# First head group of an attention and FFN kernel: keys and queries in two loads each, scores and exponentials by pairs of heads

## The chip, the cores and the metric

The kernel runs on one core of a Trainium2 chip. The metric is the device time of one execution in microseconds (us). Three executions of the kernel before took 380.77, 381.61 and 380.28; the median is 380.77.

The engines of the core go by these names in the profile: PE is TensorE (matmuls; PEld are its weight loads), DVE is VectorE, ACT is ScalarE, POOL is GpSimd, which here mostly issues loads, and SP is SyncE, which issues most stores.

## The reference

Attention without a mask over 8 batches, 12 heads, 448 tokens and 64 columns per head, and then a two-layer FFN with a SiLU between its layers (768 to 2048 to 768):

```python
def _attn_ref(q, k, v):
    scale = 1.0 / np.sqrt(q.shape[-1])
    scores = scale * np.matmul(q, k.transpose(0, 1, 3, 2))
    scores = scores - np.max(scores, axis=-1, keepdims=True)
    attn = np.exp(scores)
    attn = attn / (np.sum(attn, axis=-1, keepdims=True) + 1e-09)
    return np.matmul(attn, v).astype(np.float32)

def _moe_ref(x, w_in, w_out):
    h = x @ w_in
    g = h * (1.0 / (1.0 + np.exp(-h)))
    return (g @ w_out).astype(np.float32)

# x = attention's output, tokens by heads x columns: (3584, 768)
```

Inputs and output are float32. The kernel computes in fp16 and leaves out the maximum, since the inputs are small.

## The kernel before, in words

**Tiling of the attention.** Heads go in groups of four (HG = 4), so a batch has three groups and the program 24 units (n = 0 to 23). A group's raw keys form one tile of 128 rows: each head takes 32 rows, and each row holds 14 tokens of 64 columns. Raw queries have the same form. POOL loads them with a cast to fp16 (`load_k`, L316; `load_q`, L324; 224 KB each as fp16). VectorE then turns them: its transposes of 32 x 32 blocks bring the columns of a head onto that head's 32 rows (`turn_k` with three instructions, L387 and L390; `turn_q`, L402, in place). The queries of unit 0 are loaded and turned in two pieces of seven tokens each (PIECES).

**Scores and exponentials.** A score matmul (`score`, L438) contracts over the 32 rows of one head. The matmuls of four heads lie on four different row strips of the PE array. Scores of one chunk of 128 keys and four heads (a burst) go to two PSUM buffers, y = 0 for heads 0 and 1 and y = 1 for heads 2 and 3. There are three such buffers (`s_ring`). ScalarE takes one buffer at a time through the exponential (`expo`, L483 and L494: 128 x 896), which frees it. The last chunk has only 64 keys, so a burst of "rest rows" holds those of two units: unit 0's fourth burst needs the turned keys and queries of unit 1 as well.

**Sums and products.** For the first units, row sums and products with V are matmuls on 32-column strips (`attend_alone`, L544): part 0 is the sums, parts 1 and 2 the products for the two halves of the head's columns. VectorE inverts the sums (L616, L624, L631) and normalizes the products (L661), which frees their PSUM bank; at the start there are two such banks. V comes in four loads (L344), each of which writes 32 rows.

**The FFN.** Once all heads of a batch are normalized, FFN1 runs (`times`, L673), then tanh on ScalarE, the gate on VectorE and FFN2. For later batches, FFN work fills TensorE between score bursts. It uses the full array, or, when a matmul on column strips stands before it and attention is still to come, four matmuls on strips of 32 columns in place of one.

**What sets the order.** The program carries its own planner. `Order.step` goes through time with assumed durations and hands VectorE and ScalarE, whenever they are free, the ready piece of work of the lowest rank and time plus bias; `rank` puts a bias of -9 or less ahead of all others. TensorE's next piece is chosen in the loop at the end (L1880 on): scores from `qk_seq`, sums and products from `av_seq`, FFN work from `moe`. Where TensorE would stand idle in the opening, the loop puts in matmuls on zeros (L1872), the first time as many as FIRST says. The instructions are issued in the planned order, and on the chip semaphores do the waiting. Loads are issued by POOL in a fixed list (`plan_k`, `plan_q`, `plan_v`, `plan_w_in`, `plan_w_out`, L1039 on); a load waits until its buffer is free (two raw-key buffers, four raw-query buffers). The planner's constants for loads (DMA_SLOW, `few`) count how many have been sent.

**What the change touches.** `load_k`, `load_q`, `turn_k`, `turn_q`, `scores`, the planning of loads (`plan_q`, the list at L1039) and of turns (`plan_turn`), the sequence `qk_seq` (L1603), and the readiness and issue of a burst (`qk_at`, `run_qk`).

## Time and profile before

| What | Value |
|---|---|
| Median of three executions | 380.77 us |
| Profiled execution, its own time | 380.37 us |
| Its span, first to last instruction | 378.6 us |
| Granted TensorE clock | 1.000 |
| TensorE busy | 372.4 us (98%) |
| VectorE, ScalarE, POOL busy | 269.7, 255.5, 84.9 us |
| Read from HBM, written to HBM | 45.61 MB, 11.01 MB |
| First load issued, first key turn begins | 1.25, 5.04 us |
| First scores, first exponential | 6.15, 6.76 us |
| First FFN matmul | 23.95 us |

How to read it: the busy time of a matmul group runs from its first start to its last end and can hold waits in between. The chain of work that ended last is followed back from the last instruction, at each step to what released it; its pieces are those whose length makes up the span. A timeline line gives start, length, engine, line, operation, output<-inputs, shapes and count, and in brackets the idle time before it and what ended that.

### The profile page before, as it was taken

To read this page: it belongs to the slowest core of one execution; us is meant where nothing else is said; L and a number is where in the kernel's file an instruction comes from. 1 tells how busy PE (TensorE), PEld (TensorE's weight loads), DVE (VectorE), ACT (ScalarE), POOL (GpSimd) and SP (SyncE) were. 2 spreads that over 40 slices of the span, in tenths; PEclk is the share of its full clock that TensorE was granted. 3 is DMA by queue.
4 is the path that set the end of the run, shared out by engine and by line. 5 is a ranking of instruction groups with operands and counts; after the bars stand their busy time and mean duration, and the time that the engine had idled before them with its cause. 6 is when DMAs were issued, how large, how long until landed. Compare 5 with 4: busy or idle time off the path is not lost.

```text
span 378.6 us, 9949 instructions
## 1 busy us (share of the span) xinstructions
PE 372.4 (98%) x4024; PEld 191.5 (51%) x4024; DVE 269.7 (71%) x553; ACT 255.5 (67%) x400; POOL 84.9 (22%) x155
## 2 busy tenths in 40 slices
PE   7999999999999999999999999999999999999995
PEld 3367664444444444444444454545555555556663
DVE  3666859899995869995969998898475424446541
ACT  4988874897768787877788777658872238882221
POOL 6652438451007326006423200000000000000000
PEclk9999999999999999999999999999999999999999
DMA  7999999946139948148955421200002331002343
GB/s 120 191 208 210 206 204 186 190 53 98 17 92 124 184 49 124 26 94 116 170 86 73 54 53 34 68 18 0 3 1 59 94 74 26 0 2 59 84 110 83
DMA packets 35854, 34.47 MB, mean 91 GB/s; under 512 B 11872, under 2 KB 35040, under 8 KB 35808
## 3 DMA queue, kind: packets, MB, share of 16 engines
q0 software_dynamic: 25312, 22.82, 40.3%
q1 hardware_dynamic: 10080, 10.53, 10.6%
q8 instruction: 31, 0.51, 0.5%
q10 hardware_dynamic: 416, 0.49, 0.4%
q14 instruction: 15, 0.12, 0.1%
HBM read 45.61 MB, written 11.01 MB: 150 GB/s over the span
## 4 chain that ended last, share of the span: by engine, by line
PE 97%; DMA 1%; ACT 1%; DVE 0%; issue 0%; POOLq 0%
PE p L673 32%; PE h L673 21%; PE f L673 16%; PE s L438 12%; PE a L558 8%; PE o L673 3%; PE a L544 2%; PE a L591 2%; DMA rk<-in_k_dram 1%; ACT T L483 1%; PE z L1872 0%; PE z L673 0%; PE z L544 0%; DVE KT L387 0%; ACT ost L977 0%
## 5 line engine op out<-in xcount | busy, mean ns | idle before, releaser
L494 ACT ACTIVATE E<-s 128x896 f16<-128x896 f32 x164 | 142.0, 923 | 23.7 <-PE s L438 23.6
L673 PEld LDWEIGHTS <-w_in_t 128*128 128x128 f16 (+1 forms) x981 | 61.3, 97 | 45.2 <-issue 8.4
L673 PE MATMUL h<-xT,w_in_t 128*32 128x448 f16 (+2 forms) x834 | 84.0, 333 | 0.0
L344 POOL DMA_DIRECT2D V<-in_v_dram x88 | 48.4, 557 | 52.5 <-PE a L558 32.2
L673 PEld LDWEIGHTS <-G 128*128 128x128 f16 (+1 forms) x637 | 43.4, 97 | 32.4 <-issue 5.2
L977 ACT COPY ost<-p 128x384 f32<-128x384 f32 x52 | 24.9, 479 | 50.4 <-PE p L673 31.9
L705 ACT ACTIVATE th<-h 128x448 f16<-128x448 f32 x67 | 36.6, 546 | 22.8 <-PE h L673 19.1
L673 PE MATMUL p<-w_out_t,G 128*128 128x384 f16 (+1 forms) x343 | 51.9, 326 | 0.0
L438 PE MATMUL s<-rq,KT 32*128 32x448 f16 (+3 forms) x728 | 45.4, 347 | 1.3 <-DVE rq L402 1.0
L983 DVE TENSOR_TENSOR ost<-p,ost 128x384 f32<-128x384 f32 x39 | 21.6, 553 | 31.3 <-PE p L673 14.3
L673 PEld LDWEIGHTS <-S 128*128 128x128 f16 (+1 forms) x330 | 29.5, 98 | 23.5 <-issue 4.2
L673 PE MATMUL p<-D,S 128*128 128x384 f16 (+1 forms) x214 | 37.5, 326 | 0.0
L558 PE MATMUL a<-E,V 128*32 128x448 f16 (+1 forms) x640 | 32.9, 356 | 0.0
L749 DVE SCALAR_TENSOR_TENSOR G<-th,h 128x448 f16<-128x448 f16 (+1 forms) x52 | 28.8, 565 | 4.5 <-ACT th L705 3.9
L324 POOL DMA_DIRECT2D rq<-in_q_dram x25 | 13.8, 553 | 67.3 <-PE s L438 57.7
L661 DVE SCALAR_TENSOR_TENSOR xT<-a,rdn 128x448 f16<-128x448 f32 x46 | 27.0, 618 | 2.7 <-PE a L558 2.0
L438 PEld LDWEIGHTS <-KT 32*128 32x128 f16 (+1 forms) x824 | 12.5, 96 | 30.3 <-issue 28.1
L507 DVE TENSOR_TENSOR T<-T,E 128x1792 f16<-128x1792 f16 x20 | 21.7, 1086 | 3.9 <-ACT E L494 3.8
L876 DVE TENSOR_TENSOR p<-f,p 128x448 f32<-128x448 f32 x15 | 9.4, 624 | 20.4 <-PE f L673 13.5
L673 PE MATMUL f<-sx,tw 128*128 128x448 f16 x102 | 23.5, 352 | 0.0
L507 DVE TENSOR_TENSOR T<-E,E 128x1792 f16<-128x1792 f16 x20 | 21.6, 1082 | 2.5 <-ACT E L494 2.5
L558 PEld LDWEIGHTS <-V 128*32 128x32 f16 (+1 forms) x640 | 13.7, 95 | 18.0 <-issue 10.3
(95 smaller groups left out, 430.2 us busy)
## 6 DMA issues: line engine op xcount, KB each, us to landing
out_dram<-ost SPq DMA_DIRECT2D x194, 48.0 KB, 1.6
rk<-in_k_dram POOLq DMA_DIRECT2D x24, 224.0 KB, 5.0
rq<-in_q_dram POOLq DMA_DIRECT2D x23, 224.0 KB, 5.6
w_out_t<-in_moe_w_out_dram POOLq DMA_DIRECT2D x4, 768.0 KB, 12.5
V<-in_v_dram POOLq DMA_DIRECT2D x42, 64.0 KB, 4.1
V<-in_v_dram POOLq DMA_DIRECT2D x42, 48.0 KB, 4.3
w_in_t<-in_moe_w_in_dram POOLq DMA_DIRECT2D x6, 256.0 KB, 9.0
w_in_t<-in_moe_w_in_dram POOLq DMA_DIRECT2D x3, 512.0 KB, 12.3
```

What stands on the lines that cost most here:

```text
L324: nc.gpsimd.dma_start(out=rawq[n][:, cols], in_=group_of(q, b, hg)[:, cols])
L344: nc.gpsimd.dma_start(out=VT[b][32 * x : 32 * (x + 1), hs, at : at + count, :], in_=v[b, hs].rearrange("h (i g) d -> i h g d", g=TPP)[:, : ...
L438: nc.tensor.matmul(out=pS[p0 : p0 + 32 * (x1 - x0), h % 2, at : at + q1 - q0], lhsT=KT[(b, hg)][32 * h : 32 * (h + 1), key_rows(b, hg, c, ...
L494: nc.scalar.activation(out=E[(n, w)][:, 2 * y : 2 * y + 2, :], in_=pS_t[(n, w, y)][:, :, 0:S], func=AF.Exp, scale=attn_scale,)
L507: nc.vector.tensor_tensor(out=T[n], in0=T[n] if step else E[(n, 0)], in1=E[(n, step + 1)], op=ALU.add,)
L558: nc.tensor.matmul(out=a[32 * h : 32 * (h + 1), 0:S], lhsT=VT[b][k0:k1, HG * hg + h, place(b, hg, c), part - 1 :: 2], rhs=e[k0:k1, h], sta ...
L661: nc.vector.scalar_tensor_tensor(out=x3(b, cc)[:, cc % 3, 32 * g0 : 32 * g1], in0=acc[(n, part)][:, 0:nq], scalar=0.5, in1=rdn_t[n].rearra ...
L673: nc.tensor.matmul(out=out[i : i + cut], lhsT=w[:, i : i + cut], rhs=x, start=start, stop=stop, skip_group_check=True,)
L705: nc.scalar.activation(out=th, in_=h_t[(b, f, t0)][:, 0:n], func=AF.Tanh)
L749: nc.vector.scalar_tensor_tensor(out=dst[:, f, at + lo : at + hi], in0=th_t[(b, f, t0)][:, lo - t0 : hi - t0], scalar=1.0, in1=h_t[(b, f, ...
L977: nc.scalar.copy(out=ost(qd, *OUT[m]), in_=bank(qd, BANK[m]))
L983: nc.vector.tensor_tensor(out=t, in0=bank(qd, BANK[m]), in1=t, op=ALU.add)
```

## The change

The keys and the queries of the first head group are each loaded in two halves of 64 rows (two heads each), in the order keys, queries, keys, queries; before, it was one key load and two query loads of 128 rows. The turns of this group are made half by half, with the queries still in two pieces of tokens: ten transposes on 64 rows in place of five on 128. The first three bursts of unit 0 are split by y: the three for heads 0 and 1 come first, then the three for heads 2 and 3. The fourth burst stays whole. The turns of units 1 to 3 get a bias of -11 in place of 20, and so rank ahead of most of VectorE's work; those of unit 0 get 18 and 19. The first run of zero matmuls is given as 40 and not 47 units of 128 columns, and the planner's constants for loads count one load more.

The order that the planner makes differs in three places. In the opening, TensorE issues the scores as told above; the first product of unit 0 with V, which stood between the second and the third burst of unit 1, comes behind the third; and the turn of unit 2's queries comes ahead of unit 0's first normalization on VectorE. From the first scores of batch 2 to the FFN of that batch, score bursts come later among the FFN pieces, and more of the first FFN2 rows are done on column strips (14 more blocks). From there to the end TensorE's order is the same. The core of the diff:

```diff
-                took += DMA_SLOW if len(self.sent) == 3 else 0.0
-                few = len(self.sent) < 7
+                took += DMA_SLOW if len(self.sent) == 4 else 0.0
+                few = len(self.sent) < 8
...
-    COLD, FIRST, QUIET = 8.5, 47, 0.16
+    COLD, FIRST, QUIET = 8.5, 40, 0.16
...
+    def load_k(b, hg, h0=0, h1=HG):
+        if h0 == 0:
+            rawk[(b, hg)] = sb.tile([128, TPP * D], FP16, name=f"rk_{b}_{hg}", tag="rk", bufs=NRK)
+        rows = slice(32 * h0, 32 * h1)
+        nc.gpsimd.dma_start(out=rawk[(b, hg)][rows], in_=group_of(k, b, hg)[rows])
...
+    def turn_k(b, hg, h0=0, h1=HG):
+        rows = slice(32 * h0, 32 * h1)
+        t = rawk[(b, hg)][rows].bitcast(FP32).rearrange("p (g i) -> p g i", i=32)
...
+    def turn_q(n, g0, g1, h0=0, h1=HG):
+        rows = slice(32 * h0, 32 * h1)
+        t = rawq[n][rows].bitcast(FP32).rearrange("p (g i) -> p g i", i=32)[:, g0:g1]
...
-                for h in range(HG):
+                for h in [2 * y + i for y in ys for i in range(2)]:
...
-    plan_k(0, 0)
-    plan_q(0)
+    first_ld = {}
+    for i in range(2):
+        for fn, ring, x in ((load_k, rk_ring, (0, 0)), (load_q, rq_ring, (0,))):
+            first_ld[(i, fn)] = od.load(
+                64,
+                2 * D * TPP,
+                lambda fn=fn, x=x, i=i: fn(*x, 2 * i, 2 * i + 2),
+                None if i else ring,
+            )
...
+    def turn_bias(n):
+        return -11 if n <= 3 else 20
...
+    def plan_first_turns():
+        kt_ring.take()
+        for i in range(2):
+            heads = (2 * i, 2 * i + 2)
+            fn = lambda heads=heads: turn_k(0, 0, *heads)
+            then = rk_ring.give if i else None
+            kt_op[("half", i)] = od.add(
+                Op("DVE", 0.73, fn, [first_ld[(i, load_k)]], 18 + i, then=then)
+            )
+            for x, (g0, g1) in enumerate(PIECES):
+                fn = lambda heads=heads, g0=g0, g1=g1: turn_q(0, g0, g1, *heads)
+                op = Op("DVE", 0.13 + (g1 - g0) / 30.0, fn, [first_ld[(i, load_q)]], 18 + i)
+                qt_op[("half", i, x)] = od.add(op)
+        kt_op[(0, 0)] = kt_op[("half", 1)]
+        qt_op[0] = [qt_op[("half", i, x)] for i in range(2) for x in range(2)]
...
-                qk_seq += [([n], w, (0, 1)) for w in range(len(BURSTS[n]))]
+                if n == 0:
+                    qk_seq += [([0], w, (y,)) for y in range(2) for w in range(3)]
+                    qk_seq.append(([0], 3, (0, 1)))
+                else:
+                    qk_seq += [([n], w, (0, 1)) for w in range(len(BURSTS[n]))]
...
-            for x in {0 if c == NCH - 1 else i for c, i in BURSTS[n][c]} if n == 0 and c < 2 else ():
-                turns = [kt_op.get(units[0][:2]), *qt_op.get(0, [None] * 2)[x : x + 1]]
+            if n == 0 and c < NCH - 1:
+                y = ys[0]
+                turns = [kt_op.get(("half", y))]
+                turns += [qt_op.get(("half", y, x)) for x in {i for _, i in BURSTS[0][c]}]
```

## The prediction

> **What bounds the kernel now.** I read the page first, for who is busy and whose work ended last:
>
> ```profile
> PE 372.4 (98%) x4024; PEld 191.5 (51%) x4024; DVE 269.7 (71%) x553; ACT 255.5 (67%) x400; POOL 84.9 (22%) x155
> PE 97%; DMA 1%; ACT 1%; DVE 0%; issue 0%; POOLq 0%
> ```
>
> TensorE is 97% of the chain. What this change can win therefore lies before TensorE's work becomes continuous, or in the amount of that work. Second, the chain in order of time (start, length, what), for the opening:
>
> ```profile
> 1.25 3.77 DMA rk<-in_k_dram
> ...
> 5.04 0.38 DVE KT L387
> ...
> 5.81 0.30 DVE rq L402
> ...
> 6.15 0.63 PE s L438 x16
> 6.78 2.52 ACT T L483 x3
> ...
> 23.90 0.22 PE z L1872
> 24.11 1.22 PE z L673 x12
> ```
>
> The first key load sets the first turn (the VectorE transpose of raw keys or queries), the turn the first scores, these the first exponential; at 24.11 the first FFN matmul starts, and behind it every piece of the chain is TensorE at full length. Third, the timelines of ScalarE and TensorE up to there:
>
> ```profile
> 6.76 3.35 ACT L483 ACTIVATE T<-s 128x896 f16<-128x896 f32 x4 [4.74 <-PE s L438]
> 9.97 9.86 ACT L494 ACTIVATE E<-s 128x896 f16<-128x896 f32 x12
> 20.34 3.35 ACT L494 ACTIVATE E<-s 128x896 f16<-128x896 f32 x4 [0.51 <-PE s L438]
> ```
>
> ```profile
> 10.39 1.17 PE L438 MATMUL s<-rq,KT 32*64 32x448 f16 x16
> 13.96 0.82 PE L438 MATMUL s<-rq,KT 32*128 32x448 f16 x8
> 14.71 0.56 PE L544 MATMUL a<-T,V 128*32 128x448 f16 x8
> 15.58 0.81 PE L438 MATMUL s<-rq,KT 32*128 32x448 f16 x8
> 17.28 0.74 PE L438 MATMUL s<-rq,KT 32*128 32x224 f16 x16
> ```
>
> Sixteen exponentials run without a gap from 6.76 to 19.83, one every 0.80: ScalarE bounds this stretch. The scores at 13.96 and 15.58 take 0.8, while later eights take 0.57 (25.97): they wait for one of three score buffers. At 20.34 ScalarE waits for scores, so from about 17.3 TensorE bounds. Last, transfer rates in stretches of the opening (busy times, clock, DMA share, GB/s):
>
> ```profile
> 7.50:8.00 0.50, 0.44 (x14) 0.27 (x13) 0.00 (x0) 0.50 (x2) 0.50 (x2) 1.00 1.14 197
> 11.00:12.00 1.00, 1.00 (x15) 0.42 (x15) 0.69 (x3) 1.00 (x2) 0.71 (x1) 1.00 1.38 162
> ```
>
> Loads are queued back to back. The first stretch is full 128-row loads, the second V loads of 32 rows.
>
> **The change part by part.** The sum is made against the profiled execution, 380.37 (span 378.6 and 1.8 around it); it lies 0.4 under the median 380.77, and I carry the difference over to the median.
>
> *First loads.* The 224 KB key load took 3.77 from issue. Half of it saves 112 KB; at the 160 to 190 GB/s of 3.5 to 5.0 us that is 0.60 to 0.70. Bounds: nothing (all latency) to 0.7; I take 0.62, as full loads that follow each other are spaced by their bytes. Keys of heads 0 and 1 land at 4.40. Their queries, second in the queue, have 112 KB less ahead than the first query piece had (1.93 + 3.6 = 5.5) and land at 4.9. The second pair ends at the same byte as before, by 6.9, as the last query piece did.
>
> *Turns.* Three key transposes took 0.69 up to the query's start (5.04 to 5.73), the first query piece 0.37 and 0.05 to the score. No row has 64-row transposes; bounds are half and the same, and I take the same, since length follows the columns. 4.42 + 0.69 + 0.42 gives scores at 5.53, not 6.15. The second set adds some 1.5 us to VectorE, which idles 0.83 and 1.41 there; it ends by 7.65, ahead of the next keys at 8.75.
>
> *Scores by pairs.* Sixteen matmuls on four row strips took 0.58; eight on two strips keep two strips empty. Bounds 0.29 and 0.58; I take 0.58, as each strip does as much as before. First exponential at 5.53 + 0.61 = 6.14: 0.62 earlier. It hides the doubled score time: each burst of 0.58 is shorter than one step of 0.80.
>
> *What is late next.* The second pair: turned by 7.3, scored by 7.95, due at 6.14 + 3 x 0.80 = 8.54, so 0.6 spare. The fourth burst mixes in head group 1, whose query is turned only at 9.85 + 0.65 = 10.50; before, that was hidden by the buffer that came free at 9.97 + 0.93 = 10.9. Its first half now ends near 11.1, where 10.94 is due; before, it was used at 11.56. So ScalarE keeps 0.46 of the 0.62.
>
> *POOL and the queue.* One more DMA issue (0.56), and the load of group 2's keys waits for a raw-key buffer, free when the second half is turned (about 6.7, before 6.10). V, queries 2 and everything behind are issued 0.6 to 0.9 later. Cover: the data queued ahead; V needed 5.3 to 6.1 to land against 3.77 for an empty queue, so over 1.5 us of backlog. If the cover went, V lands at 15.2 to 15.5 instead of 14.6.
>
> *TensorE's new order.* In the built program the first attention product of group 0 moves behind the last score burst of group 1. That burst waits for a buffer: the eleventh exponential ends at 9.97 + 6 x 0.81 + 0.95 = 15.7, now 15.25. It ends at 15.6; then two products (0.87 and 0.8) and the scores of group 2 (0.5) end at 17.75 against 18.02. So only about 0.25 of the 0.46 reaches the FFN. Bounds: -0.62 (all of it), and +0.45 if the first landing does not move and the product, which filled that wait, still follows it.
>
> *Turns ranked first.* The turn of queries 2 moves ahead of a normalization on VectorE (16.05 and 16.59 before). Queued behind it are that normalization, which frees a bank for the next sums at 17.75, and keys (1,0). The load lands at about 15.7 (6.7 from issue) and the product to be normalized ends at 16.45, so it costs nothing; if the load lands after 16.5, that lateness passes on.
>
> *Fillers.* Twelve first zero matmuls become ten; the last ones ran 0.22 apart (four in 0.98 from 4.15), so they end at about 4.7 against scores at 5.53, less idle than the 1.02 before. Nothing.
>
> *Later.* From the scores of batch 2 (61.95) to batch 2's FFN the order differs, then it is the same to the end. Switches between full, row-strip and column-strip work fall from 181 to 177. Sixteen output matmuls take 2.71 in the chain and twelve 2.06: 0.1625 each, so 0.11 of the 2.06 is the switch. Four fewer: -0.44. Fourteen more blocks in column strips cost the same: eight took 1.30 = 8 x 0.1625. Bounds -0.5 and +0.8 (one exponential, 0.92, laid bare where scores now come later; nearest row: no TensorE wait in 61.95 to 105, so I add 0.1).
>
> Sum: -0.25 - 0.44 + 0.1 = -0.6: 379.8 for the profiled execution, 380.2 as median.
>
> **Rivals.** *Half-rate halves (slower).* If a 64-row load takes as long as a 128-row one, the four first loads need about 5.0 us of data time and not 2.5, and everything queued behind lands 2.5 later. Group 1's queries land at 12.3, are turned at 13.0, and the seventh exponential starts at 13.6 and not 11.56: +2.0, with +1.6 left after the switches: 382.4. It begins to cost once the four loads need 0.5 more than 2.5 (11.56 less 11.1). Against it: 32-row loads ran at 162, 128-row ones at 197 GB/s. [...]
>
> *No earlier landing (no change).* The 3.77 is latency; the exponentials start where they did, the moved product costs 0.45, the switches return 0.44: 380.8. For it: 1.25 to about 2.5 shows no data at all. Against: later loads are spaced by bytes.
>
> *All of it arrives (faster).* The full 0.62 holds, the scores of group 2 lose the 0.45 that the weight load waited for the turn of queries 2 at 17.27, and the switches give 0.44: -1.5, 379.3. Against it: the buffer wait in front of the moved product.
>
> **How the numbers follow.** Chances: forecast 0.42, no earlier landing 0.17, all of it 0.27, half rate 0.14. A measurement of this kernel tells about 0.3% (1.14 us) from no change. Forecast and no earlier landing lie within it: 0.59; faster 0.27; slower 0.14. The range runs from 378.9 (379.3 less the 0.4 between profile and median) to 382.0 (380.8, +0.8 of the later bound, +0.4), leaving out most of half rate; the forecast's own is 379.4 to 381.0.
>
> **What would show it.** Right: key landing near 3.15 from issue, first exponential near 6.1, the seventh near 11.1, first FFN matmul near 23.9 (24.11 less 0.25), and the same gap from there to the end less 0.4. Wrong: a first exponential after 6.5; group 1's queries landing after 10.2; a TensorE wait before the product of group 0 for V, or between 62 and 105.

## The result, and the profile after

The change makes the kernel slower by about 1.5 us. Eleven executions of each kernel gave medians of 380.62 us before (380.14 to 381.61) and 382.09 us after (381.50 to 383.30); the ratio is 1.0038, 95% interval 1.0026 to 1.0049. The forecast was 380.2, with a range up to 382.0. The profiled execution after took 382.04 us with a span of 380.3, against 380.37 and 378.6: 1.67 more.

Of the page after, the busy times and the shares of the chain:

```profile
PE 372.9 (98%) x4063; PEld 192.0 (50%) x4063; DVE 271.8 (71%) x558; ACT 255.8 (67%) x400; POOL 85.5 (22%) x156
PE 94%; DMA 3%; POOL 1%; DVE 1%; issue 0%; ACT 0%; POOLq 0%
```

TensorE has hardly more to do (372.9 against 372.4), but 3% of the chain is now transfers, where it was 1%. The chain after, in order of time (start, length, what), shows which:

```profile
2.44 4.18 DMA rk<-in_k_dram
...
6.64 0.64 DVE KT L392 x2
7.28 0.14 DVE KT L396
7.42 0.28 issue
7.70 0.54 POOL rk L318
8.24 1.79 POOL V L345 x3
...
10.70 0.54 POOL rq L325
11.24 8.16 DMA rk<-in_k_dram
...
19.42 0.64 DVE KT L392 x2
20.06 0.12 DVE KT L396
20.18 0.52 DVE xT L668
20.70 0.04 issue
20.74 0.94 PE a L551 x16
...
26.14 1.21 PE z L680 x12
```

The first FFN matmuls of this view start at 26.14, before at 24.11. The chain does not run through the first half of the keys at all. It runs through the second half, which took 4.18 us and landed at 6.62; through its turn, which gives POOL the raw-key buffer back; through POOL's list of loads behind that; through the keys (1,0), the first group of batch 1, 8.16 us in flight; and through their turn, behind which a normalization waits on VectorE, and behind that a product on TensorE.

ScalarE's timeline after (start, length, engine, line, operation, in brackets the idle time before and what ended it):

```profile
5.85 1.73 ACT L490 ACTIVATE T<-s 128x896 f16<-128x896 f32 x2 [3.82 <-PE s L445]
7.46 0.92 ACT L501 ACTIVATE E<-s 128x896 f16<-128x896 f32 x1
8.67 1.73 ACT L490 ACTIVATE T<-s 128x896 f16<-128x896 f32 x2 [0.29 <-PE s L445]
10.28 0.92 ACT L501 ACTIVATE E<-s 128x896 f16<-128x896 f32 x1
11.91 1.73 ACT L501 ACTIVATE E<-s 128x896 f16<-128x896 f32 x2 [0.71 <-PE s L445]
13.87 5.04 ACT L501 ACTIVATE E<-s 128x896 f16<-128x896 f32 x6 [0.23 <-PE s L445]
19.27 1.73 ACT L501 ACTIVATE E<-s 128x896 f16<-128x896 f32 x2 [0.36 <-PE s L445]
22.36 3.35 ACT L501 ACTIVATE E<-s 128x896 f16<-128x896 f32 x4 [1.37 <-PE s L445]
```

Before, sixteen exponentials ran from 6.76 without a gap. Now the first starts 0.91 earlier, but there are four gaps in the sixteen, and the gap behind them is 1.37 instead of 0.51. A gap costs a little more than its length, because the next start otherwise comes before the last end: 0.80 from start to start, 0.92 for one alone. How late each exponential starts, against the kernel before, gives the whole account (from the two timelines; the last column is the first FFN matmul, 25.98 less 23.95):

```
exponential     1      2      4      7      9     11     13     15     17    FFN
after       -0.91  -0.92  -0.50  +0.35  +0.71  +0.81  +0.82  +1.29  +2.03  +2.03
```

Nothing that is lost in one step is won back in a later one. The steps are -0.92 (up to the third), +0.42 (second pair of heads), +0.85 (the fourth burst, which needs group 1's queries), +0.47 (ninth to eleventh), +0.47 (the first scores of group 2) and +0.74 (the scores behind the held product): +2.03 at the first FFN matmul. From there to the end the kernel is 0.36 faster (354.29 against 354.65), which leaves 1.67. TensorE's waits in the same stretch are few:

```profile
8.06 1.36 PE L445 MATMUL s<-rq,KT 32*128 32x224 f16 x20 [0.75 <-DVE rq L409]
10.95 0.95 PE L445 MATMUL s<-rq,KT 32*64 32x448 f16 x15 [0.62 <-DVE rq L409]
16.53 0.57 PE L445 MATMUL s<-rq,KT 32*128 32x448 f16 x6 [0.15 <-ACT E L501]
20.74 0.94 PE L551 MATMUL a<-E,V 128*32 128x448 f16 x16 [0.64 <-DVE xT L668]
```

Each has a turn, and so a load, or ScalarE behind it; the last one has a normalization that stands behind a turn. Three stretches of the opening (length, busy times, granted clock, DMA share, GB/s), the kernel before first and then the kernel after:

```profile
7.00:8.00 1.00, 0.94 (x18) 0.54 (x18) 0.34 (x1) 1.00 (x2) 1.00 (x3) 1.00 1.09 194
9.00:10.00 1.00, 0.85 (x9) 0.22 (x7) 0.66 (x4) 1.00 (x3) 0.84 (x3) 1.00 1.27 192
12.00:13.00 1.00, 1.00 (x10) 0.21 (x8) 0.00 (x0) 1.00 (x2) 0.72 (x1) 1.00 1.45 168
```

```profile
7.00:8.00 1.00, 0.31 (x3) 0.03 (x1) 0.81 (x5) 1.00 (x2) 0.30 (x1) 1.00 0.92 131
9.00:10.00 1.00, 1.00 (x11) 0.32 (x5) 0.76 (x3) 1.00 (x2) 1.00 (x2) 1.00 0.76 63
12.00:13.00 1.00, 1.00 (x7) 0.25 (x9) 0.76 (x3) 1.00 (x2) 1.00 (x2) 0.50 1.35 180
```

The transfers run at 131 and 63 GB/s where the kernel before had 194 and 192 in the same stretches (between them, from 8 to 9, it is 172 against 190). From 12 to 13 TensorE had half its clock, which the kernel before never had there.

### The profile page after: what moved, and what is told of

Same layout as the page of the kernel before. It is cut to its first block, busy times and chain, and to the rows that moved or that the text cites. A ratio compares the mean times of both kernels' runs of the same rounds, so it can differ in the third digit from the quotient of the medians.

```text
span 380.3 us, 10027 instructions
## 1 busy us (share of the span) xinstructions
PE 372.9 (98%) x4063; PEld 192.0 (50%) x4063; DVE 271.8 (71%) x558; ACT 255.8 (67%) x400; POOL 85.5 (22%) x156
## 4 chain that ended last, share of the span: by engine, by line
PE 94%; DMA 3%; POOL 1%; DVE 1%; issue 0%; ACT 0%; POOLq 0%
PE p L680 32%; PE h L680 21%; PE f L680 16%; PE s L445 10%; PE a L565 8%; DMA rk<-in_k_dram 3%; PE o L680 3%; PE a L551 2%; PE a L598 2%; POOL V L345 1%; DVE KT L392 0%; PE z L680 0%; POOL rk L318 0%; POOL rq L325 0%; DVE xT L668 0%
```

## The experiments

Sixteen kernels were run. First the readings that all of them share, one profiled execution each. That execution is not always near the median: it took the lowest time of its kernel in E1, E2, E6, E10 and E14 and the highest in E4, E5 and E15. A load counts as landed when its last part has: the trace has 16 landing events for each load. The first two tables are worked out from those events and from the transfer records. "All first" is the last landing of the first group's keys and queries, k1 and q1 are the keys and queries of group 1, V is the last of the four V loads, and MB is what had been moved by 8 us. Times in us.

```
four first loads                  first   all first   k1     q1     V      MB
the changed kernel                 4.12     7.57      9.13  10.23  16.11  0.72
E1  before, four 64-row loads      4.19     7.11      9.67  10.79  16.07  0.75
E2  before, four column loads      4.34     7.83      9.27  10.34  16.02  0.72
E5  changed, no buffer wait        4.23     7.38     10.13  11.23  15.89  0.76
E6  changed, two exchanged         4.13     7.81      9.73  10.83  16.65  0.75
E7  changed, products first         4.17     7.70      9.33  10.40  16.57  0.76
E15 as E6, fewer weights           4.17     7.40      9.18  10.26  16.70  0.78
E16 changed, fewer weights         4.11     7.44      8.82  10.07  17.03  0.75
mean                               4.18     7.53      9.41  10.52

three first loads                 first   all first   k1     q1     V      MB
the kernel before                  5.02     6.91      8.73   9.83  14.62  0.86
E3  before, POOL held up           4.88     6.29      7.60   9.29  14.09  0.89
E8  before, ranks                  4.80     7.68      9.35  10.47  15.23  0.86
E9  before, no buffer wait         4.58     6.91      8.03   9.13  14.29  0.89
E10 before, more weights           4.80     6.71      8.27   9.36  14.19  0.87
E11 changed, whole loads           4.60     6.76      7.99   9.07  16.18  0.89
E12 E11, old ranks                 5.04     6.70      8.37   9.50  15.66  0.86
E13 E11, no buffer wait            4.92     6.50      8.45   9.53  14.42  0.85
E14 E11, neither                   5.11     7.11      8.70   9.78  14.76  0.84
mean                               4.86     6.84      8.39   9.55
```

The first landing comes 0.68 earlier with four loads, and everything behind it later: the last of the first group by 0.69, group 1's keys and queries by 1.0. By 8 us, 0.72 to 0.78 MB had been moved with four loads and 0.84 to 0.89 with three: no profile of one kind lies within the other. The landings of group 1 overlap (queries at 10.07 to 11.23 with four loads, 9.07 to 10.47 with three).

**E1: four first loads, and nothing else.** The kernel before, with its loads alone split into halves of 64 rows:

```diff
+        if (b, hg) == (0, 0):
+            load_rows(rawk[(0, 0)], k, 0)
+            load_rows(rawq[0], q, 0)
+            return
...
+        if n == 0:
+            load_rows(*((rawq[0], q) if g0 else (rawk[(0, 0)], k)), 1)
+            return
```

> The kernel before, every instruction in its old order on every engine; only the first key load and the two first query loads are issued as four loads of 64 rows (keys, queries, keys, queries). No pairs in turns, scores or exponentials, so the first turn of keys needs both key halves. Theory 'the queue runs dry' (a half is 0.62 us of data and POOL needs about 0.55 per issue, so the transfers start from an empty queue again and again): the second key half lands near 6.6, as in the changed kernel, not near 5.0; the first exponential starts near 8.3 instead of 6.76; the first raw-key buffer is given back some 1.5 later, the loads behind it are issued 1.5 later, and the first FFN matmul comes 1.2 to 1.8 later than 23.95: 381.9 to 382.5. Rival 'bytes only' (my prediction's step: the second pair ends at the same byte as one whole load): second key half near 5.6, first exponential near 7.4, 0.3 to 0.7 later in all: 381.0 to 381.4. Rival 'half rate' (64 rows at half the rate): data of the first two halves takes 1.25 us each, the second key half lands after 7.5: over 383.

Measured: 383.02 (381.75 to 383.84), ratio 1.0073 (1.0056 to 1.0090). The first exponential came at 8.28 and the first FFN matmul at 25.46, 1.52 and 1.51 later than before; all sixteen exponentials in between were late by the same 1.5. The second key half landed at 6.10 and the second query half at 7.11. Half rate is out: the data of all four halves was there by 7.11, not after 7.5 for the third alone. The second key half lies between the two other theories (5.6 and 6.6), but group 1's loads came as late as in the changed kernel, which "bytes only" doesn't explain. "The queue runs dry" had the first exponential (8.3) and the loss at the FFN (1.2 to 1.8) right, but not the second key half or the time; no view shows a queue without data. Since all sixteen exponentials are late by the same amount, this profile's loss arises at its first landing, and group 1's late loads cost nothing more here. The profile (381.75) had a mean granted clock of 0.999; the other five executions had 0.991 to 0.996 and took 382.44 to 383.84, so that about half of the median's loss isn't in the profile.

**E2: the same with 128 rows.** As E1, but each half has 128 rows and half the columns:

```diff
-        rows = slice(64 * i, 64 * i + 64)
-        nc.gpsimd.dma_start(out=t[rows], in_=group_of(src, 0, 0)[rows])
+        cols = slice(D * TPP // 2 * i, D * TPP // 2 * (i + 1))
+        nc.gpsimd.dma_start(out=t[:, cols], in_=group_of(src, 0, 0)[:, cols])
```

> The kernel before, its order untouched; its first keys and queries come as four loads (keys, queries, keys, queries) as in the run with 64-row halves, but each of 128 rows and half the columns: the same bytes, count and order, other partitions. In the profiles with 64-row halves group 1's keys landed at 9.1 to 10.1 and its queries at 10.2 to 11.2; with the old three loads at 8.0 to 9.4 and 9.1 to 10.5. Theory 'the fourth load and its issue put the transfers back': landings as with 64-row halves, queries of group 1 after 10.2, 382 to 383. Rival 'transfers to 64 partitions are the slow ones': keys of group 1 at 8.0 to 8.9 and queries at 9.1 to 10.0; the first turn still waits for the third load, so that the first exponential comes at 7.2 to 8.0 and the time is 381 to 382.

Measured: 382.59 (382.00 to 382.97), ratio 1.0048 (1.0035 to 1.0061). Group 1's queries landed at 10.34 and its keys at 9.27, nearer to the means with four loads (10.52 and 9.41) than with three (9.55 and 8.39), and 0.72 MB by 8 us is less than any kernel with three loads had moved. So 64 partitions are not the reason: split by columns over all 128 partitions, the first loads still had group 1's keys 0.88 and its queries 0.79 behind the means with three.

**E3: POOL later, and no fourth load.** Two fills on POOL (0.71 us together) between the third load and the fourth of the kernel before:

```diff
+        if (b, hg) == (0, 1):
+            for _ in range(2):
+                nc.gpsimd.memset(G[0:64, 0, 0:256], 0.0)
```

> The kernel before with two small zero fills on POOL (64 x 256, some 0.6 us together, into a tile that is idle then) between the third and the fourth load; loads, bytes and orders are the same. It makes POOL issue group 1's keys and queries as late as the fourth first load does in the kernels with half loads, without a fourth load. Theory 'the issue is what counts': group 1's queries land 0.5 to 1.0 later than the 9.1 to 10.5 (mean 9.6) of the eight profiles with three first loads, near 10.4, as in the six with four (10.2 to 11.2, mean 10.6); 380.6 to 381.3. My prediction's step (data queued ahead covers a later issue) and the rival 'the additional load itself, in the transfer engines': they land at 9.1 to 10.0, and the time stays 380.2 to 380.6.

Measured: 380.52 (380.11 to 381.39), ratio 1.0000 (0.9991 to 1.0008). Group 1's keys were issued at 3.66 (2.99 before; 3.45 in the changed kernel) and landed at 7.60, its queries at 9.29. A later issue by itself costs nothing while three loads stand in the queue, as the prediction had said. So the delay of the four-load kind does not come from the later issue of group 1's loads. E3 leaves the first three loads as they were; whether few bytes in the queue ahead of them matter, it doesn't test.

**E4: one first load fewer.** The first queries in one load:

```diff
-        cols = slice(D * g0, D * g1)
+        if n == 0 and g0:
+            return
+        cols = slice(D * g0, D * (g1 if n else TPP))
```

> The kernel before with one first load fewer: the first queries come in one load, not in two pieces; bytes and orders are the same. The first scores then wait for the whole query load (5.6 to 6.4, not 5.5). Theory 'each load costs by itself, whatever its bytes': group 1's keys and queries land 0.4 to 1.0 earlier than with three loads (queries at 8.6 to 9.3), while the first exponential comes 0.3 to 0.8 later than 6.76; the sixteen exponentials hide the earlier landings, so the time is 380.6 to 381.3. Rival 'bytes alone set the later landings': queries of group 1 at 9.4 to 10, the same time.

Measured: 381.21 (381.03 to 381.96), ratio 1.0015 (1.0006 to 1.0024). Keys of group 1 landed at 8.23 and queries at 9.43, within the spread of the kernels with three loads: "each load costs by itself" is not borne out from three to two, in one profile. What the fourth load does cannot be taken for a price per load.

**E5: no wait for the raw-key buffer.** The changed kernel, its first raw keys in a tile that is idle then:

```diff
-            rawk[(b, hg)] = sb.tile([128, TPP * D], FP16, name=f"rk_{b}_{hg}", tag="rk", bufs=NRK)
+            rawk[(b, hg)] = (
+                G[:, 0] if (b, hg) == (0, 0) else sb.tile(...)
+            )
...
-        for fn, ring, x in ((load_k, rk_ring, (0, 0)), (load_q, rq_ring, (0,))):
+        for fn, ring, x in ((load_k, None, (0, 0)), (load_q, rq_ring, (0,))):
...
-            then = rk_ring.give if i else None
+            then = None
```

> The changed kernel, but the first head group's raw keys lie in a tile that is idle at that time, so that the load of group 2's keys waits for no raw-key buffer on POOL's queue (3.14 us in the changed kernel, 2.02 before). Theory 'the buffer wait makes everything behind late': group 2's keys are issued near 4.6 instead of 7.70, V, queries 2 and keys (1,0) each 1.5 to 3 earlier, keys (1,0) land before 18; the first FFN matmul comes 1.2 to 2 earlier than 25.98: 380.0 to 380.9. Rival 'the late second halves alone' (the queue runs dry at 4 to 5.5 us and stays behind by those bytes, the wait is hidden): the transfers start earlier but land no earlier, since they follow the same bytes: 381.7 to 382.1. Rival 'pairs and order' (the loss is in TensorE's and VectorE's order): 382.1.

Measured: 382.02 (381.11 to 382.61), ratio 1.0042 (1.0026 to 1.0058): no better. POOL issued group 2's keys at 4.50 instead of 7.70, but group 1's queries landed at 11.23, a full 1.0 later than in the changed kernel, so that ScalarE stood idle for 1.94 ahead of the seventh exponential. V came only 0.2 earlier.

**E6: the second normalization ahead of the turn of keys (1,0).** One exchange on VectorE, TensorE's order untouched: the turn is put into the program 0.7 later than planned.

```diff
-    def emit(self, fn):
-        self.out.append((self.now, len(self.out), fn))
+    def emit(self, fn, later=0.0):
+        self.out.append((self.now + later, len(self.out), fn))
...
-        self.emit(op.emit)
+        self.emit(op.emit, getattr(op, "later", 0.0))
...
+            if n == 3:
+                kt_op[(b, hg)].later = 0.7
```

> The changed kernel with one pair of instructions on VectorE exchanged: the second normalization ahead of the turn of keys (1,0), which waits for its load until 19.39. TensorE's order is the same. Theory 'the ranked turn passes the lateness of its load on': TensorE's wait of 0.64 ahead of the product at 20.74 goes, the first FFN matmul comes 0.5 to 0.7 earlier: 381.3 to 381.6. Rival 'TensorE would have to wait for those keys anyway' (the scores of keys (1,0) need the turn a little later, and the wait only moves there): 381.9 to 382.1.

Measured: 382.43 (381.90 to 382.88), ratio 1.0053 (1.0039 to 1.0067). In the profile the wait of 0.64 is gone and the first FFN matmul starts at 25.11, 0.87 earlier than in the changed kernel, yet the span is only 0.2 shorter and the median no better. From there to the end it takes 355.01, 0.72 more than the changed kernel. The last weights, which landed at 57.95, account for 0.14 of that: TensorE's order reached them at 57.85 and went on at 57.99. Where the rest went is not shown.

**E7: the products ahead of the last burst.** One constant of the planner, LATE, from -0.3 to 1.2, with which both products of group 0 stand ahead of the last score burst of group 1 on TensorE, and the normalizations ahead of the ranked turns on VectorE:

```diff
-    NEAR, LATE = 0.15, -0.3
+    NEAR, LATE = 0.15, 1.2
```

> The changed kernel with one constant of the planner changed so that, on TensorE, the first attention products of group 0 stand ahead of the last score burst of group 1 and, on VectorE, the two normalizations stand ahead of the turns that rank first; the loads stay. Theory 'the transfers are late and bound both TensorE's start and the weights': the order is immaterial, at most the 0.64 in front of the product at 20.74 goes, and the weights then land no earlier than 57.9: 381.7 to 382.2. Rival 'the moved product is the loss' (my own upper bound of 0.45 for it, and more): 381.4 or less.

Measured: 382.45 (382.24 to 383.96), ratio 1.0051 (1.0033 to 1.0070). V landed at 16.57, and TensorE waited with those scores behind it:

```profile
16.82 0.56 PE L551 MATMUL a<-T,V 128*32 128x448 f16 x8 [1.92 <-DMA V<-in_v_dram]
```

The thirteenth exponential was 2.71 late, and the first FFN matmul came at 26.53. With V this late, the moved product protects the scores.

**E8: the ranks alone, on the kernel before.**

```diff
-    lambda: turn_k(b, hg), [ld_k[(b, hg)]], 20, then=rk_ring.give
+    lambda: turn_k(b, hg), [ld_k[(b, hg)]], -11 if 0 < n <= 3 else 20, then=rk_ring.give
...
-                    20,
+                    -11 if 0 < n <= 3 else 20,
```

> The kernel before with loads and TensorE's order untouched; only the turns of head groups 1 to 3 rank ahead on VectorE as in the changed kernel: the turn of queries 2 ahead of the first normalization, the turn of keys (1,0) ahead of the second. Theory 'a turn ranked ahead blocks the normalization behind a late load': keys (1,0) land at 17.86 here, so the second normalization waits for that turn (0.7 long, done by 18.6) and the product it makes room for, at 18.72 before, moves by 0 to 0.4: 380.6 to 381.1. My prediction's step says that it costs nothing: 380.6. Rival 'the ranks are most of the loss': 381.5 or more.

Measured: 380.39 (380.09 to 381.14), ratio 0.9999 (0.9989 to 1.0009). Where loads land about as before, the ranks show no cost.

**E9: the kernel before without its own buffer wait** (POOL waited 2.02 ahead of 6.10), by the edit of E5.

> The kernel before, but the first head group's raw keys lie in a tile that is idle then, so that POOL's wait of 2.02 us for a raw-key buffer ahead of the load at 6.10 goes and 2 us of loads stand in the queue earlier. Loads, turns and TensorE's order stay. Theory 'more loads in the queue make the earlier ones land later' (in the changed kernel without that wait, group 1's queries landed at 11.23, not 10.23): group 1's queries land 0.5 to 1.4 later than 9.83, ScalarE waits for their scores, 380.7 to 381.5. Rival 'transfers are served in order': group 1's queries land at 9.8, what is behind lands up to 0.3 earlier, 380.1 to 380.5.

Measured: 380.37 (380.17 to 381.30), ratio 0.9996 (0.9982 to 1.0010). Queries of group 1 landed at 9.13: more loads in the queue do not by themselves make the earlier ones late. As far as one profile each can tell, what E5 showed belongs to the four-load opening.

**E10: additional weights on the kernel before.**

```diff
     def load_w_out(f0, f1):
+        if f0 == 0:
+            nc.gpsimd.dma_start(out=w_out_t[:, 12:13], in_=...)
```

> The kernel before, with one load of 192 KB of weights made twice: an additional transfer, issued ahead of the first load of the second FFN weights at 26.4, and nothing else. It measures what late transfers cost when nothing before 26 us is touched. Theory 'the stream of weights is a second bound, 0.2 us behind TensorE': the additional 0.95 us of transfer makes the weights that land at 56.21 land near 57.15, TensorE, which takes them at 56.39, waits for 0.6 to 0.8: 380.9 to 381.2. Rival 'the weights have cover': no wait of TensorE, 380.3 to 380.5.

Measured: 381.06 (380.60 to 381.94), ratio 1.0011 (0.9998 to 1.0024), some 0.4 us by the ratio, which the interval does not tell from nothing. The profile, the lowest of the twelve, takes 0.41 more from the first FFN matmul to the end (355.06 against 354.65). Of this, 0.18 is a wait for V at 44.1 and 0.16 the wait that was expected, smaller since the weights landed at 56.62:

```profile
56.66 1.48 PE L678 MATMUL o<-w_out_t,G 128*32 128x384 f16 x32 [0.16 <-DMA w_out_t<-in_moe_w_out_dram]
```

The stream of weights is thus close behind TensorE until 57 us (in the kernel before, weights that landed at 56.21 were taken at 56.39).

**E11: the changed kernel with whole first loads.** Keys of 128 rows and two query pieces, as before, and with them the planner's constants for loads; the rest of the change stays:

```diff
-    for i in range(2):
-        for fn, ring, x in ((load_k, rk_ring, (0, 0)), (load_q, rq_ring, (0,))):
-            first_ld[(i, fn)] = od.load(64, 2 * D * TPP, ...)
+    whole_k = od.load(128, 2 * D * TPP, lambda: load_k(0, 0), rk_ring)
+    for x, (g0, g1) in enumerate(PIECES):
+        first_ld[("q", x)] = od.load(128, 2 * D * (g1 - g0), ...)
```

> The changed kernel with the three whole first loads of before (keys of 128 rows, two query pieces by columns); turns by half tiles, scores and exponentials by pairs of heads and the ranks on VectorE stay as in the changed kernel. Theory 'the four half loads put the transfers behind' (0.33 MB less had been moved by 20 us, and neither the landings nor the weights behind them catch up): landings as in the kernel before (group 1's queries near 9.8, last weights for TensorE near 56.2), the first FFN matmul back to 23.7 to 24.4: 380.0 to 380.7. Rival 'pairs and ranks cost by themselves': the landings come back and the time does not, 381.5 or more.

Measured: 383.05 (382.73 to 384.02), ratio 1.0062 (1.0037 to 1.0087), far from what I expected. The landings of group 1 came back (9.07), the time did not. Three runs take this kernel apart, in a square of two causes.

**E12, E13, E14: whole loads, with the old ranks, without the buffer wait, and with both edits.** The ranks go by one line, the buffer as in E5:

```diff
     def turn_bias(n):
-        return -11 if n <= 3 else 20
+        return 20
```

> The changed kernel with whole first loads, and with the ranks of before on VectorE (no turn ahead of a normalization); POOL still waits for the raw-key buffer. Same theory: V lands late (15.3 to 16.2) and TensorE waits for it for 0.5 to 1, but no normalization stands behind a turn: 381.0 to 382.0. Rival 'the ranks are the loss': 380.0 to 380.7. Rival 'late transfers alone': 382.6 or more, as with the ranks.

> The changed kernel with the three whole first loads of before, and its first raw keys in a tile that is idle, so that POOL does not wait for the raw-key buffer. The run with whole loads and that wait gave 383.05: group 1's queries landed at 9.07, but POOL issued V 0.9 later than before, V landed at 16.18 (before 14.62) and the turn of queries 2, ranked ahead, held the first normalization until 17.3. Theory 'the buffer wait makes loads late and the ranks pass it on': V lands at 14.2 to 14.7, nothing ahead of a normalization waits, first FFN matmul 23.6 to 24.4: 379.9 to 380.7. Rival 'the ranks cost by themselves': 381.8 or more.

> The changed kernel with whole first loads, without the buffer wait and with the ranks of before: of the change only the half-tile turns and the scores and exponentials by pairs of heads are left. Theory: both causes are gone, 379.9 to 380.6, and if the later part of the kernel keeps the 0.3 that the changed kernel gained there, at the lower end. Rival 'scores by pairs cost by themselves' (bursts of two strips, 16 matmuls in two parts): 381.3 or more.

Measured: E12 382.95 (382.66 to 383.49), ratio 1.0057 (1.0045 to 1.0069); E13 382.31 (381.60 to 384.68), ratio 1.0045 (1.0027 to 1.0063); E14 382.71 (381.54 to 384.51), ratio 1.0053 (1.0030 to 1.0076). In all three my theory said less, and each measured time lies where one of the rivals had it. E14 holds only half-tile turns, scores and exponentials by pairs and the order that follows from them (it also lacks the buffer wait, which by E9 costs the kernel before nothing); its loads landed like those of the kernel before, and still its first FFN matmul came at 25.21, 1.26 late. Its timelines show where, ScalarE first (the profile took 381.54, the lowest of the seven; what the others lost beyond that is not shown):

```profile
6.84 0.92 ACT L498 ACTIVATE T<-s 128x896 f16<-128x896 f32 x1 [4.81 <-PE s L453]
8.37 0.92 ACT L498 ACTIVATE T<-s 128x896 f16<-128x896 f32 x1 [0.61 <-PE s L453]
...
17.75 3.35 ACT L509 ACTIVATE E<-s 128x896 f16<-128x896 f32 x4 [0.36 <-PE s L453]
```

```profile
14.76 0.82 PE L453 MATMUL s<-rq,KT 32*128 32x448 f16 x8
15.51 0.56 PE L559 MATMUL a<-T,V 128*32 128x448 f16 x8
...
16.28 0.55 PE L559 MATMUL a<-T,V 128*32 128x448 f16 x8
...
17.14 0.57 PE L453 MATMUL s<-rq,KT 32*128 32x448 f16 x8
```

The second exponential is 0.79 late: by pairs it needs the second query piece, turned for heads 0 and 1 only, where by bursts the second exponential was that of heads 2 and 3 on the first piece. With whole loads that piece landed at 7.11, and its turn also had the second key half ahead of it on VectorE. The thirteenth is 1.40 late, 0.59 more: both products stand between the last two score bursts of group 1, where the kernel before had one (scores at 15.58 there, at 17.14 here). So scores by pairs with whole loads are no gain, and the planner's order around the products has a price without any late load. Since E11 to E14 order the products as E7 does, they don't price the pairs in the changed kernel's own order.

In E13 V landed at 14.42 and the loss was still 2.01 at the first FFN matmul; there TensorE also had half its clock from 10.50 to 13.91. The ratios of the four runs of the square lie between 1.0045 and 1.0062, and their intervals overlap: neither the buffer wait nor the ranks is the loss. The wait is not free, though: E11 and E12, which have it, also show TensorE waits of some 0.5 us each at 37 to 45 us, for V and for FFN weights, and E13 and E14 show none there.

**E15, E16: the exchange of E6 and the changed kernel, each with fewer weights.**

```diff
+    nc.vector.memset(w_out_t[:, 6:8], 0.0)
...
     def load_w_out(f0, f1):
+        f1 -= 2 * (f0 == 4)
```

Both leave out weights that the result needs. The fill with zeros takes VectorE 0.70 from 2.21 on, ahead of its first turn.

> The changed kernel with the second normalization ahead of the turn of keys (1,0), as in the run that gave 382.43, and with half of the second load of the second FFN weights left out (0.39 MB; zeros stand in their place), so that all weights behind it land some 1.9 earlier. Theory 'the exchange on VectorE gains 0.9 by the first FFN matmul (25.11 instead of 25.98) and gives it back because the last weights land at 57.95': without that the gain stays, 381.0 to 381.6. Rival 'the exchange gains nothing, the profiled run was a good one': 382.0 to 382.6.

> The changed kernel itself with the same half load of weights left out. It is the control of the run before: TensorE took the last weights at 58.29, 0.3 after they landed, so TensorE's own path is the later of the two and the time stays: 381.7 to 382.2. If the late weights are most of the loss by themselves: 381.2 or less.

Measured: E15 382.24 (381.42 to 382.31), ratio 1.0032 (1.0019 to 1.0044); E16 382.14 (381.93 to 382.91), ratio 1.0041 (1.0028 to 1.0054). The weights were out of the way (landed at 56.14 and 56.70), and the exchange still brought nothing that can be told. E15's profile shows what took its place, on VectorE and then ScalarE:

```profile
18.90 0.65 DVE L411 STREAM_TRANSPOSE rq<-rq 128x448 f32<-128x448 f32 x1 [2.72 <-DMA rq<-in_q_dram]
19.46 0.58 DVE L670 SCALAR_TENSOR_TENSOR xT<-z,rdn 128x448 f16<-128x448 f32 x1
```

```profile
11.61 6.58 ACT L503 ACTIVATE E<-s 128x896 f16<-128x896 f32 x8 [0.40 <-PE s L447]
20.21 1.73 ACT L503 ACTIVATE E<-s 128x896 f16<-128x896 f32 x2 [2.02 <-PE s L447]
```

Here group 1's queries were turned early enough for the seventh exponential to be level with the kernel before (+0.04), and then the queries of unit 2 landed at 18.87, their turn held the first normalization, and the fifteenth exponential was 2.24 late. In E16 it was V at 17.03: -0.13 at the fourteenth, +1.56 at the fifteenth.

E16 keeps the order of the changed kernel's opening and had the full clock in it, so it also shows what the half clock cost there (TensorE, then ScalarE):

```profile
10.79 0.60 PE L447 MATMUL s<-rq,KT 32*64 32x448 f16 x15 [0.59 <-DVE rq L411]
11.42 6.59 ACT L503 ACTIVATE E<-s 128x896 f16<-128x896 f32 x8 [0.34 <-PE s L447]
```

The fifteen score matmuls that took 0.95 in the changed kernel (10.95) took 0.60 here (0.61 in E7), and eight exponentials follow without a gap, where the changed kernel lost 0.47 from the seventh to the thirteenth. So in the changed kernel's profile some 0.35 of the seventh exponential's lateness and the 0.47 behind it belong to the half clock. It is not what makes the kernel slower as such: of its eleven executions, five had a mean granted clock of 0.999 or 1.000 and took 381.51 to 382.21, median 382.00, against 380.62 before; the six with 0.993 to 0.996 took 381.50 to 383.30, median 382.60.

How late the exponentials started, against the kernel before:

```
exponential              1      4      7     13     15     17    FFN
the changed kernel   -0.91  -0.50  +0.35  +0.82  +1.29  +2.03  +2.03
E5  no buffer wait   -0.80  -0.69  +1.39  +2.14  +2.65  +2.57  +2.57
E6  two exchanged    -0.41  -0.26  +0.61  +0.62  +1.16  +1.08  +1.16
E7  products first   -0.86  -0.38  +0.18  +2.71  +2.70  +2.58  +2.58
E15 as E6, lighter   -0.58  -0.50  +0.04  +0.06  +2.24  +2.15  +2.27
E16 lighter          -0.87  -0.63  -0.14  -0.13  +1.56  +1.92  +1.92
E1  loads alone      +1.52  +1.51  +1.51  +1.51  +1.52  +1.52  +1.51
E14 pairs alone      +0.08  +0.81  +0.81  +1.40  +1.39  +1.26  +1.26
E8  ranks alone      +0.23  +0.42  +0.41  +0.46  +0.44  +0.39  +0.39
```

In every kernel with pairs and four loads the early start is used up by the fifteenth exponential, each time in another place: at group 1's queries, at V, at the queries of unit 2, and behind it at the keys (1,0). Where one is early or taken away, the next late load is there. This is read from the waits. No kernel that was run has the changed kernel's order with loads that land as before, so that taking the late loads away would give the time back is not shown. No version that was run beats the kernel before; E8, E9 and E3 equal it.

## Why the prediction was wrong, by its steps

- **First loads: half right, and the step that failed.** The first half lands 0.68 earlier in the mean (0.62 was taken), at 4.12 in the profiled execution (4.40). "The second pair ends at the same byte as before, by 6.9": it ended at 7.57, at 7.53 in the mean of eight profiles against 6.84 with three loads, and group 1's loads came 1.0 later. E1 and E2 show that the split alone does this and that the number of rows does not; E3, that the later issue of group 1's loads does not.
- **Turns: right.** Three transposes of 64 rows took 0.75 (4.14 to 4.89), those of 128 rows 0.76 (9.16 to 9.92, group 1); the first scores came at 5.24 (5.53).
- **Scores by pairs: right for the first exponential,** 0.61 after the scores, at 5.85 (6.14). E14 shows a price that the step did not see, an early need of the second query piece; in the changed kernel that piece comes with the first half, and the second exponential is on time.
- **What is late next: the terms were mis-sized.** The spare 0.6 of the second pair became a wait of 0.29. Group 1's queries were turned by 10.90, not 10.50, and the seventh exponential started at 11.91, not 11.1; of these 0.8, 0.4 is the turn and some 0.35 the half clock of the scores (E16). The 0.46 that ScalarE should have kept is a loss of 0.35.
- **POOL and the queue: wrong in size, and the cover did not reach.** Issues behind the second half were 1.6 later, not 0.6 to 0.9, since the buffer comes free only when the late second half is turned. V landed at 16.11, beyond the 15.2 to 15.5 that the step gave for the case that the cover goes. E3 shows that the cover is real for a later issue alone; what failed is the transfers ahead, which had moved 0.14 MB less by 8 us (0.72 against 0.86).
- **TensorE's new order: mis-sized.** The step let the gain shrink from 0.46 to 0.25, a loss of 0.21; from the thirteenth to the fifteenth exponential 0.47 was lost, about the upper bound (0.45). E7 shows that both products ahead of that burst are no better here. In the working, 9.97 + 6 x 0.81 + 0.95 is 15.78, not 15.7; the profile before has that end at 15.67, so nothing hangs on it.
- **Turns ranked first: the condition came true.** "If the load lands after 16.5, that lateness passes on": unit 2's queries landed at 17.26 and keys (1,0) at 19.39; 0.74 at the seventeenth exponential. E8 shows no cost of the ranks where loads are early.
- **Fillers: the wait ahead of the first scores was shorter, as taken (0.34 against 1.02), but the sum has no term for the clock.** It was half from 11.03 to 14.45 in the profile, and E16 puts that at some 0.8 of the lateness. Executions with the full clock were still 1.4 slower in the median.
- **Later: right.** -0.34 was taken and -0.36 is what the two profiles give from the first FFN matmul to the end (354.29 against 354.65). E5 and E7, with the same later order, have 354.32 and 354.30; E1, E8 and E9, with the old one, 354.51 to 354.56.

The sum was -0.6; read off step by step it is -0.92 + 0.42 + 0.85 + 0.47 + 0.47 + 0.74 - 0.36 = +1.67, by which the profiled executions differ. Of the rivals, half rate has fallen with E1 and E2, although the time that it gave, 382.4, was the nearest, by luck; "no earlier landing" has fallen with the first exponential. The error behind the step was to cost the second half by its bytes, and then to treat the waits behind it as separate, each with its own cover. By the waits, they hang on one stream of loads, and when that is 1 us behind, each cover goes in turn. That the second half and group 1's loads land late because of the split is shown by E1 and E2; that these landings, and not the pairs or the order, are the loss of the changed kernel is read from its waits and remains open, since E11 to E14 with whole loads were no faster.

## What to carry to other kernels

Before the first load of a stream is split to win its first landing, price what lands last: here 0.7 us at the first landing was paid for with 0.7 at the end of the same data and 1.0 for the next group's loads. Where a chain of equal steps runs without a gap, tabulate how late each step starts against the kernel before: the loss is read off step by step, and a step whose lateness never shrinks has no slack behind it. And where removing one wait brings no time, look for the next late input of the same stream before the theory is dropped or the wait is called harmless.

## What the runs showed of the hardware that was not expected

The same bytes in four loads instead of three are moved later: 0.72 to 0.78 MB against 0.84 to 0.89 by 8 us. In the transfer records, packets of 2 to 9 us that took over 0.3 us were 34 to 51 in the kernels with four loads and 20 to 41 with three, which overlap (most packets of 1792 bytes took 0.154). It is not rows (E2), not a later issue of the loads behind (E3) and, from three loads to two, not the number alone (E4). How much is queued in the first microseconds is not ruled out: the fourth load, which completes the first 448 KB, was issued at 2.94, and the third of three at 2.47. What makes the transfers slow is open.

What used a load began after the last of its 16 parts. In the changed kernel the parts of group 1's keys landed between 7.06 and 9.13 and their turn began at 9.16, the parts of its queries between 8.88 and 10.23 with the turn at 10.25; in E5 the parts of the keys landed between 7.00 and 10.13. In single profiles one part alone was late, in one load after another: in the changed kernel 15 of 16 parts of the keys (1,0) were there at 18.38 and the last at 19.39, of the queries behind them at 19.40 and 20.37, of the weights behind those at 21.01 and 21.69; in E16 15 of 16 parts of the last V load were there at 15.76 and the last at 17.03. Whether that is why some kernels vary more (three of E14's executions took 383.68, 384.26 and 384.51, the others 381.54 to 382.71) is not shown.

TensorE's clock fell to half for 3.41 us in the opening of four of the profiles: the changed kernel (11.03 to 14.45), E4, E5 and E13. The longest wait of TensorE ahead of it was 0.75 in the changed kernel and 1.93 in E4. E7, with waits of 0.82, 0.66 and 1.92, kept the full clock (0.999 in the mean of its profile), and so did E1 with one of 1.48 (0.999), so the length of a wait alone does not decide it. What does is not shown.
